# Attention scores of a pair of heads on the two row halves of TensorE, with q and k split once per pair

## The chip, the cores and the metric

The kernel runs on one core of one Trainium2 chip. The metric is the device time of one execution in microseconds (us); the time before is the median of three runs. TensorE (PE in the profile) multiplies, VectorE (DVE) and ScalarE (ACT) do elementwise work, and SyncE (SP) issues every transfer between HBM and the core.

## The reference, cut to what matters

```python
# batch 4, 8 heads, seq 768, head dim 64; sink 4, window 128
scores = scale * np.matmul(q, k.transpose(0, 1, 3, 2))
keep = is_sink | in_window                  # a band of 128 keys, and the first 4 keys
a = softmax(np.where(keep, scores, -1e9))
x = np.matmul(a, v)                         # (3072, 512) once the heads lie side by side
h = x @ w_in                                # 512 -> 2048
g = np.where(h >= 1, h, np.where(h <= -1, 0, (h + 1) ** 2 / 4))
x = g @ w_out                               # 2048 -> 512
logits = x @ phi                            # 32 slots; softmax over tokens, over slots
slots = softmax_over_tokens(logits).T @ x
out = softmax_over_slots(logits) @ experts(slots)     # 8 experts, w1 and w2
```

## The kernel before

**Attention** is cut into 96 steps m: 12 groups g of 256 query rows (3 to a batch), in each group 4 pairs of heads hp, in each pair 2 query tiles t of 128 rows. The pair number is k = 4g + hp = m // 2. A step makes a 128x272 score tile for each of its two heads a (16 sink keys and two blocks of 128 keys; 128x128 for the first tile of a batch): `st_s` on PE, `st_ttr` (mask and row minimum) on DVE, `st_exp` on ACT, a norm, transposes `st_pt`, and for each pair one `st_pv` that sums with V. In steps from FO on, `st_fold` adds one half of the band into the other, so that two transposes do instead of four and DVE, not ACT, copies them out.

**Scores.** q and k of a head come by one transfer into a `qkr` tile (64 rows of data; the array in HBM holds them twice, one copy under the other). For pairs with k < WH (9 before) a head's scores are one plain float32 matmul on the 64 rows, which the trace shows as two records (L490, "s<-qkr 64*128"). For the others the head is split: `qkh` holds the rounded high part of q and k on rows 0 to 63, and on rows 64 to 127 the low part of q beside the high part of k once more; `kl` holds the low part of k on all 128 rows. Then a head takes two single-pass matmuls over all 128 rows (L494 and L495). The split costs for each head a copy on ACT or DVE (`sp_hi`, L461 or L463) and two subtractions on DVE (`sp_ql` and `sp_kl`, both recorded at L292).

**MLP.** Unit n (96 of them) is one 128-row tile times one 512-wide block of w_in: `u_mm` (twelve 128x512 matmuls, L633), `u_r` on ACT, `u_a` and `u_g` on DVE, transposes `u_gt` (L659), and the logits `u_lg` (L678). w_in and w_out arrive as 64-bit words and are unpacked on ACT and DVE during the first 140 us. The experts follow as a tail of some 74 us.

**Order.** `Plan` simulates the engines with a planned cost for each step, and the order in which its steps start is the order of each engine's queue. `Plan.setup` charges PE a set-up of 0.15 or 0.2 when it goes from or to steps named in PARTS (those that use 32 or 64 columns of the array); steps s are not in PARTS. Where the plan sees PE without work before the first logits, or near the end, `filled` puts fill matmuls (L1380). A score tile takes one of two PSUM banks "S", given back by `st_exp`.

Of the kernel before, what the change touches and what calls it, by code (L numbers as in the profile page):

```python
# [172 lines left out]
def attn_moe_softmoe_kernel(ctx, tc, qk0, qk1, kt, qt, vt, vs, sizes,  # L173
# [117 lines left out]
    def minus(o, x, y):  # L291
        V.tensor_tensor(o, x, y, ALU.subtract)  # L292
# [117 lines left out]
    def at(shape, tag, bufs, dt=F32, nm=None):  # L410
        return att["pool"].tile(shape, dt, name=nm or tag, tag=tag, bufs=bufs)
# [5 lines left out]
    def load_qk(h):  # L417

        g, h8 = divmod(h, 8)
# [6 lines left out]
        qkr[8 * g + h8] = t  # L426
# [22 lines left out]
    def qk_tiles(hh):  # L449
        k, i = divmod(hh, 2)  # L450
        return qkh[k], kl[k], i, 528 if (k // 4) % GPB == 0 else 672

    def sp_hi(hh, e):

        k = hh // 2
        if hh % 2 == 0:
            qkh[k] = at([128, 2, 672], "qkh", 2, F32R, nm=f"qkh{k}")
            kl[k] = at([128, 2, 416], "kl", 2, F32R, nm=f"kl{k}")
        h, l, i, w = qk_tiles(hh)
        if e == "ACT":  # L460
            A.activation(h[:, i, 0:w], qkr[hh][:, 0:w], AF.Copy)  # L461
        else:
            V.tensor_copy(h[:, i, 0:w], qkr[hh][:, 0:w])  # L463

    def sp_ql(hh):
        h, l, i, w = qk_tiles(hh)
        minus(h[64:128, i, 0:256], qkr[hh][64:128, 0:256], h[64:128, i, 0:256].bitcast(F32))

    def sp_kl(hh):
        h, l, i, w = qk_tiles(hh)  # L470
        minus(l[:, i, 0:w - 256], qkr.pop(hh)[:, 256:w], h[:, i, 256:w].bitcast(F32))
# [12 lines left out]
    def st_s(m, a):  # L484
        g, hp, t, b, i, k0, n, nm = geom(m)
        k = 4 * g + hp
        s = pt([128, 512], "S", 2, nm=f"s{m}_{a}")
# [534 lines left out]
    NTW, XCAP, GCAP, RCAP, ARATE, WK0, WK1, OK0, OK1 = 7, 3, 6, 3, 0.947, -7.119, 1.613, 6.435, 1.902  # L1022
    PK0, AN0, AN1, GTO, LGO, RO, AO, PVO, PTO = 60.0, 1, 55, 2.818, 1.79, 0.87, 0.891, 1.256, 1.239
    CKO, SPO, BO, GR, LASTN, LGT, HC, SLACK, FM = 1.633, -0.108, -0.708, 14, 5, 1.124, 6, 0.044, 0.296
    CT0, CT1, QKR, WIK, HO, TWO, NPT, NEAR, WH = -1, 0.5, 3, -26, 0, 1, 3, 3, 9
    FO, PAIRED, LGD = 22, 1, 1.5
# [105 lines left out]
    def fast_path():  # L1132
# [27 lines left out]
        for k, (kind, j, c) in enumerate(pairs):  # L1160
            key = (WK0 + k * WK1) if kind == "w" else (OK0 + (k - n_w) * OK1)
            ld = op(f"ld_raw{k}", "DMA", 2.92, key - 4, cv_load, acq=["w8", "raw"])
            ab = op(f"abs{k}", "ACT", 1.06, key + BO, lambda k=k: cv_abs(k), [ld], acq=["cv"] if wide else [])
# [30 lines left out]
        lds, spl, vop, vsop = {}, {}, {}, {}  # L1194
# [12 lines left out]
        for m in range(NPAIR):  # L1207
            g, hp, t, b, i, k0, w, nm = geom(m)
            key = A_(m)
            wide_q = g % GPB != 0  # L1210
            if t == 0:
                sp = []
                for a in range(2):
                    hh = 8 * g + 2 * hp + a
                    l = op(f"ld_qk{hh}", "DMA", .66 if WHOLE(hh // 2) else .96 if wide_q else .73, key - 4, lambda hh=hh: load_qk(hh), acq=["qkr"])
                    if WHOLE(hh // 2):
                        sp.append([l])
                        continue
                    aq = ["qkh"] if a == 0 else []
                    spk = key + SPO  # L1220
                    h = op(f"qh{hh}", {"ACT": .64 if wide_q else .5, "DVE": .45 if wide_q else .37}, 0, spk,
                           lambda e, hh=hh: sp_hi(hh, e), [l], acq=aq, prior=[x[0] for x in sp])
                    q = op(f"ql{hh}", "DVE", .45, spk, lambda hh=hh: sp_ql(hh), [h])
                    kk = op(f"kl{hh}", "DVE", .6 if wide_q else .48, spk, lambda hh=hh: sp_kl(hh), [h])
                    op.free("qkr", [q, kk])
                    sp.append([h, q, kk])
                spl[g, hp] = sp
            ex, tt = [], []
            for a in range(2):
                whole = WHOLE(m // 2)  # L1230
# [3 lines left out]
                last_s = s  # L1234
# [233 lines left out]
```

## Time and profile before

| | before |
|---|---|
| median of three runs | 642.07 us (637.44 to 644.04) |
| profiled execution | 637.39 us |
| its span in the trace | 635.5 us (so 1.9 us lie around it) |
| PE busy | 616.9 us, 97% |
| DVE busy | 502.3 us, 79% |
| ACT busy | 412.3 us, 65% |

A busy PE in this profile is not a PE at its peak: a matmul's duration includes its way through the array, and matmuls overlap. What a matmul costs in a dense stream is the distance from its start to the start of the next one; that is what the rows further down are read for. PEld is PE's load of the stationary operand. In a name such as "128x512" the second number is the columns that stream; "64*128" is array rows times array columns in use.

### The profile page before, as it was taken

What the parts mean: (1) busy time and instruction counts of PE and PEld (TensorE: products, weight loads), DVE (VectorE), ACT (ScalarE), POOL (GpSimd) and SP (SyncE); (2) the same over time, 40 slices, a digit from 0 to 9 for tenths busy, and PEclk for the clock granted to TensorE, in tenths of its full rate; (3) what the DMA queues carried; (4) which work ended last, traced back from release to release, by engine and by line L of the source; (5) the groups of instructions that cost most, each with busy time, mean ns of one, the idle gap of its engine ahead of it and who ended that gap; (6) DMA issues with size and microseconds to landing.
All of it is one profiled execution on the core that took longest, in us unless ns stands there. A gap on an engine that the chain in (4) does not pass through costs nothing.

```text
span 635.5 us, 12324 instructions
## 1 busy us (share of the span) xinstructions
PE 616.9 (97%) x4420; PEld 453.3 (71%) x4420; DVE 502.3 (79%) x1561; ACT 412.3 (65%) x1175; POOL 3.3 (1%) x12
## 2 busy tenths in 40 slices
PE   8999999999999999999999999999999999999992
PEld 5667788777876778777877887886878867653452
DVE  6999999999989789878999998999998642455053
ACT  4998999888878667676776655676666433332143
POOL 0000000000000000000000000000000000010000
PEclk9999999999999999999999999999999999999997
DMA  8766384672611311421314123324230194879996
GB/s 274 231 194 218 124 281 145 219 262 99 210 47 48 112 36 36 136 65 47 104 44 122 52 64 94 88 83 132 60 109 27 36 426 154 312 300 342 418 382 221
DMA packets 34342, 100.92 MB, mean 159 GB/s; under 512 B 3808, under 2 KB 9952, under 8 KB 29664
## 3 DMA queue, kind: packets, MB, share of 16 engines
q1 hardware_dynamic: 34272, 100.04, 46.8%
q8 instruction: 37, 0.61, 0.4%
q14 instruction: 33, 0.27, 0.1%
HBM read 89.54 MB, written 10.49 MB: 157 GB/s over the span
## 4 chain that ended last, share of the span: by engine, by line


## 5 line engine op out<-in xcount | busy, mean ns | idle before, releaser
L633 PE MATMUL h<-winh,x 128*128 128x512 f32 x768 | 278.6, 407 | 0.0
L633 PEld LDWEIGHTS h<-winh,x 128*128 128x128 f32 x768 | 144.4, 188 | 34.6 <-issue 8.5
L633 PE MATMUL h<-winl,x 128*128 128x512 f32 x384 | 150.4, 392 | 0.0
L510 ACT ACTIVATE p<-s,st 128x272 f32<-128x272 f32 (+1 forms) x192 | 87.9, 463 | 24.2 <-DVE st L503 21.7
L638 ACT ACTIVATE r<-h 128x512 f32<-128x512 f32 x96 | 57.0, 595 | 48.2 <-PE h L633 27.9
L503 DVE CUSTOM_DVE_ANT_0 s<-s,nm 128x272 f32<-128x272 f32 (+1 forms) x192 | 77.6, 430 | 10.2 <-PE s L490 5.3
L633 PEld LDWEIGHTS h<-winl,x 128*128 128x128 f32 x384 | 72.6, 189 | 9.3
L666 ACT ACTIVATE gT<-gtp,one 128x512 f32<-128x512 f32 x96 | 65.7, 685 | 16.2 <-PE gtp L659 16.0
L653 DVE SCALAR_TENSOR_TENSOR gm<-r,gm 128x512 f32<-128x512 f32 x96 | 65.7, 687 | 1.1
L650 DVE TENSOR_SCALAR gm<-r 128x512 f32<-128x512 f32 x96 | 40.8, 427 | 25.0 <-ACT r L638 24.7
L659 PE MATMUL gtp<-ident_r,gm 128*128 128x128 f32 x384 | 58.7, 275 | 0.5 <-DVE gm L653 0.5
L461 ACT ACTIVATE qkh<-qkr 128x672 fp32r<-128x672 f32 (+1 forms) x61 | 44.0, 729 | 15.9 <-PE s L495 15.9
L659 PEld LDWEIGHTS gtp<-ident_r,gm 128*128 128x128 f32 x384 | 44.0, 141 | 12.3 <-issue 5.3
L598 PE MATMUL pv<-pT,v 128*64 128x128 f32 x704 | 49.0, 279 | 0.0
L494 PE MATMUL s<-qkh 128*128 128x272 f32 (+1 forms) x156 | 46.9, 318 | 0.2 <-ACT p L510 0.2
L292 DVE TENSOR_TENSOR kl<-qkr,qkh 128x416 fp32r<-128x416 f32 (+1 forms) x78 | 42.2, 541 | 0.6
L555 PE MATMUL pt<-ident_r,p 128*128 128x128 f32 x228 | 42.0, 279 | 0.2 <-ACT pT L568 0.2
L495 PE MATMUL s<-kl,qkh 128*128 128x272 f32 (+1 forms) x156 | 42.1, 287 | 0.0
L598 PEld LDWEIGHTS pv<-pT,v 128*64 128x64 f32 x704 | 37.5, 136 | 4.4 <-issue 1.6
L510 ACT ACTIVATION_READ_ACCUMULATOR p<-s,st 128x1 f32 x192 | 38.6, 201 | 0.0
L555 PEld LDWEIGHTS pt<-ident_r,p 128*128 128x128 f32 x228 | 28.4, 141 | 12.3 <-issue 3.7
L494 PEld LDWEIGHTS s<-qkh 128*128 128x128 f32 x156 | 29.4, 189 | 10.6 <-issue 8.4
(155 smaller groups left out, 933.9 us busy)
## 6 DMA issues: line engine op xcount, KB each, us to landing
w<-in_w SPq DMA_DIRECT2D x32, 1024.0 KB, 8.9
qkr<-in_qk SPq DMA_DIRECT2D x54, 336.0 KB, 3.0
raw<-in_w_in SPq DMA_DIRECT2D x8, 1024.0 KB, 6.3
raw<-in_w_out SPq DMA_DIRECT2D x8, 1024.0 KB, 6.0
qkr<-in_qk SPq DMA_DIRECT2D x24, 264.0 KB, 2.7
v<-in_vt SPq DMA_DIRECT2D x24, 256.0 KB, 3.2
out<-o SPq DMA_DIRECT2D x12, 512.0 KB, 7.0
wo<-cv SPq DMA_DIRECT2D x8, 512.0 KB, 3.4
```

Of the source, the lines that this page charges most:

```text
L292: V.tensor_tensor(o, x, y, ALU.subtract)
L461: A.activation(h[:, i, 0:w], qkr[hh][:, 0:w], AF.Copy)
L494: T.matmul(s[:, 0:n], q, qkh[k][:, a, 256 + k0:256 + k0 + n], start=True, stop=False)
L503: V.tensor_tensor_reduce(out=s, in0=s, in1=nm, op0=ALU.add, op1=ALU.min, scale=-0.125, scalar=3.0e38, accum_out=rs[m][:, a:a + 1])
L510: A.activation(p_sb[m][:, a, 0:n], s_ps.pop((m, a))[:, 0:n], AF.Exp, bias=rs[m][:, a:a + 1], scale=-1.0, accum_out=rs[m][:, 2 + a:3 + a])
L555: T.transpose(ps[:, nc_ * a + c, :], p[:, a, col:col + 128], ident)
L598: T.matmul(ps[64 * a:64 * a + 64, t, :], vch[b, ch][:, h * 64:h * 64 + 64], o[:, len(chunks) * a + c, :], start=False, stop=(c == len(chun ...
L633: T.matmul(hps[n], x[:, c, t, :], (win_h, win_l)[w][j][:, c, :], start=(k == 0), stop=(k == 11))
L638: A.activation(r, hps.pop(n), AF.Relu, bias=0.5, scale=0.5)
L653: V.scalar_tensor_tensor(gm[n], ru.pop(n), 1.0, gm[n], ALU.subtract, ALU.mult)
L659: T.transpose(ps[:, c, :], gm[n][:, c * 128:(c + 1) * 128], ident)
L666: A.activation(gT[n // 2][:, :, t * 128:t * 128 + 128], gtp.pop(n), AF.Identity, bias=one)
```

## The change

- A pair's two heads lie one under the other in HBM and in `qkr`: head 0 on rows 0 to 63, head 1 on rows 64 to 127. One transfer loads them, where there were two.
- The split is made once per pair on all 128 rows: one copy `sp_hi` into `qkh`, and one subtraction `sp_lo` of the whole width (672 or 528) into `kl`, which now holds the low parts of q and of k.
- `st_s` takes both heads in one step of PE, each on its half of the rows: high x high, high x low, low x high, for head 0 and head 1 in turn. That is six matmuls of 64 rows where there were four of 128. A step with k < WH takes one plain float32 matmul per head. The step takes both "S" banks at once.
- The plan costs a step .36 (split) or .47 (whole), where it had .251 or .46 for each head; set-up rules are as before.
- WH goes from 9 to 11, FO from 22 to 16, and the keys and limits of the plan get new values; from unit RAWN on, a place in the plan is ordered behind the last load of raw weights.

```diff
-        t = at([128, 672], "qkr", QKR, nm=f"qkr{h}")
-        w = 528 if gi == 0 else 672
-        src = qk0[b, h8 // 2, :, h8 % 2] if gi == 0 else qk1[b, gi - 1, h8 // 2, :, h8 % 2]
-        n = 64 if WHOLE(h // 2) else 128
-        SP.dma_start(t[0:n, 0:w], src[0:n])
+        t = qkr[k] = at([128, 672], "qkr", QKR, nm=f"qkr{k}")
+        SP.dma_start(t[:, 0:qk_width(k)], qk0[b, hp] if gi == 0 else qk1[b, gi - 1, hp])
...
-    def sp_ql(hh):
-        h, l, i, w = qk_tiles(hh)
-        minus(h[64:128, i, 0:256], qkr[hh][64:128, 0:256], h[64:128, i, 0:256].bitcast(F32))
-
-    def sp_kl(hh):
-        h, l, i, w = qk_tiles(hh)
-        minus(l[:, i, 0:w - 256], qkr.pop(hh)[:, 256:w], h[:, i, 256:w].bitcast(F32))
+    def sp_lo(k):
+        w = qk_width(k)
+        kl[k] = at([128, 672], "kl", 2, F32R, nm=f"kl{k}")
+        minus(kl[k][:, 0:w], qkr.pop(k)[:, 0:w], qkh[k][:, 0:w].bitcast(F32))
...
         if WHOLE(k):
-            r = qkr[2 * k + a][0:64]
-            T.matmul(s[:, 0:n], r[:, t * 128:t * 128 + 128], r[:, 256 + k0:256 + k0 + n], start=True, stop=True)
-            s_ps[m, a] = s
-            return
-        q = qkh[k][:, a, t * 128:t * 128 + 128]
-        T.matmul(s[:, 0:n], q, qkh[k][:, a, 256 + k0:256 + k0 + n], start=True, stop=False)
-        T.matmul(s[:, 0:n], q, kl[k][:, a, k0:k0 + n], start=False, stop=True)
-        s_ps[m, a] = s
+            terms = [(qkr[k], qkr[k])]
+        else:
+            terms = [(qkh[k], qkh[k]), (qkh[k], kl[k]), (kl[k], qkh[k])]
+        for x, (q, o) in enumerate(terms):
+            for a in range(2):
+                r = slice(64 * a, 64 * a + 64)
+                T.matmul(s_ps[m, a][:, 0:n], q[r, t * 128:t * 128 + 128], o[r, 256 + k0:256 + k0 + n],
+                         start=x == 0, stop=x == len(terms) - 1)
...
-                s = op(f"s{m}_{a}", "PE", (.46 if w > 128 else .22) if whole else .251, key, lambda m=m, a=a: st_s(m, a),
-                       spl[g, hp][a] + ([last_s] if last_s else []),
-                       acq=["S"], rel=["qkr"] if whole and t else ["qkh"] if t and a else [])
+            c = (.47 if whole else .36) * (1 if w > 128 else .5)
+            s = last_s = op(f"s{m}", "PE", c, key, lambda m=m: st_s(m), sp + ([last_s] if last_s else []),
+                            acq=["S", "S"], rel=["qkr" if whole else "qkh"] if t else [])
```

**Where the order moves.** First PE, in unit n = 41 (tile h_3776 before, h_3705 in the change), where a step with split heads stands between the two halves of the unit's twelve h matmuls; s_0 and s_1 are the score tiles of the two heads. Before:

```order
L633 MATMUL h_3776<-winh_264,x_3048 128x512
L494 MATMUL s_0_3793<-qkh_3633 128x128
L495 MATMUL s_0_3793<-kl_3634,qkh_3633 128x128
L494 MATMUL s_1_3798<-qkh_3633 128x128
L495 MATMUL s_1_3798<-kl_3634,qkh_3633 128x128
L633 MATMUL h_3776<-winh_264,x_3048 128x512
```

In the change, at the same place:

```order
L624 MATMUL h_3705<-winh_264,x_3018 128x512
L486 MATMUL s_0_3726<-qkh_3565 128x128
L486 MATMUL s_1_3727<-qkh_3565 128x128
L486 MATMUL s_0_3726<-kl_3570,qkh_3565 128x128
L486 MATMUL s_1_3727<-kl_3570,qkh_3565 128x128
L486 MATMUL s_0_3726<-qkh_3565,kl_3570 128x128
L486 MATMUL s_1_3727<-qkh_3565,kl_3570 128x128
L624 MATMUL h_3705<-winh_264,x_3018 128x512
```

The neighbours stay what they were; four matmuls of 128 rows have become six of 64 rows, which go to head 0 and head 1 in turn.

Second PE, in unit n = 4 (h_793 and h_796), where a step with whole heads stands between the halves. Before:

```order
L633 MATMUL h_793<-winh_607,x_305 128x512
L490 MATMUL s_0_807<-qkr_684 128x272
L490 MATMUL s_1_813<-qkr_776 128x272
L633 MATMUL h_793<-winh_607,x_305 128x512
L633 MATMUL h_793<-winl_608,x_305 128x512
```

In the change:

```order
L624 MATMUL h_796<-winh_585,x_291 128x512
L486 MATMUL s_0_811<-qkr_567 128x272
L486 MATMUL s_1_812<-qkr_567 128x272
L624 MATMUL h_796<-winh_585,x_291 128x512
L624 MATMUL h_796<-winl_586,x_291 128x512
```

The rows read alike; the two matmuls now read the upper and the lower half of one tile qkr_567, where they read the upper halves of two tiles.

Third DVE, near unit n = 40, where one pair is split (qkh_3499, kl_3500 and two qkr tiles before; qkh_3411, kl_3429 and one qkr tile in the change). Before, with other work between the rows left out:

```order
L463 CAST qkh_3499<-qkr_3412 128x528
L292 TENSOR_TENSOR qkh_3499<-qkr_3310,qkh_3499 64x256
L292 TENSOR_TENSOR kl_3500<-qkr_3310,qkh_3499 128x272
...
L292 TENSOR_TENSOR qkh_3499<-qkr_3412,qkh_3499 64x256
...
L292 TENSOR_TENSOR kl_3500<-qkr_3412,qkh_3499 128x272
```

In the change:

```order
L494 ISA s_0_3392,st_3413<-s_0_3392,nm_162 128x272
L494 ISA st_3413 128x1
L494 ISA s_1_3393,st_3413<-s_1_3393,nm_162 128x272
L494 ISA st_3413 128x1
L292 TENSOR_TENSOR kl_3429<-qkr_3040,qkh_3411 128x528
L515 TENSOR_TENSOR p_3427<-p_3427 128x2x128
```

Five instructions of DVE for the pair have become one, and the pair's one high copy stands on ACT.

## Rows read from the trace of the kernel before

**Rows 1.** Page, part 1: busy us, share of the span, instructions.

```profile
PE 616.9 (97%) x4420; PEld 453.3 (71%) x4420; DVE 502.3 (79%) x1561; ACT 412.3 (65%) x1175; POOL 3.3 (1%) x12
```

**Rows 2.** Stretches: length, busy us and instructions by engine, clock, DMA share, GB/s.

```profile
31.80:47.70 15.90, 15.90 (x88) 10.89 (x88) 15.84 (x43) 15.90 (x44) 0.00 (x0) 1.00 0.60 194
...
95.00:127.00 32.00, 32.00 (x242) 26.12 (x242) 30.27 (x85) 29.96 (x84) 0.00 (x0) 1.00 0.55 184
...
254.00:286.00 32.00, 32.00 (x226) 24.43 (x225) 25.32 (x85) 22.50 (x73) 0.00 (x0) 1.00 0.34 100
```

**Rows 3.** Waits of PE: who waited for whom, us in total, times, longest.

```profile
PE fill_lg L1380 <- DVE ident_r L230: 1.6, 1, 1.6
...
PE s L494 <- ACT p L510: 0.2, 1, 0.2
```

**Rows 4.** Timeline of PE (start us, us, what): last h of first and last unit.

```profile
44.52 0.40 PE L633 MATMUL h<-winh,x 128*128 128x512 f32 x1
...
561.16 0.40 PE L633 MATMUL h<-winh,x 128*128 128x512 f32 x1
```

**Rows 5.** Timeline of PE: a split step between gtp transposes and h.

```profile
304.44 0.60 PE L659 MATMUL gtp<-ident_r,gm 128*128 128x128 f32 x4
304.80 0.37 PE L494 MATMUL s<-qkh 128*128 128x272 f32 x1
305.01 0.29 PE L495 MATMUL s<-kl,qkh 128*128 128x272 f32 x1
305.13 0.28 PE L494 MATMUL s<-qkh 128*128 128x272 f32 x1
...
305.38 0.39 PE L633 MATMUL h<-winh,x 128*128 128x512 f32 x1
305.61 0.39 PE L633 MATMUL h<-winl,x 128*128 128x512 f32 x1
```

**Rows 6.** Timeline of PE: one whole head, then a whole step between two h.

```profile
48.94 0.72 PE L490 MATMUL s<-qkr 64*128 64x272 f32 x2
49.59 0.44 PE L589 MATMUL pv<-sTt,vs 96*128 96x128 f32 x2
...
63.62 0.40 PE L633 MATMUL h<-winh,x 128*128 128x512 f32 x1
63.95 1.18 PE L490 MATMUL s<-qkr 64*128 64x272 f32 x4
65.06 0.50 PE L633 MATMUL h<-winh,x 128*128 128x512 f32 x1
65.40 0.40 PE L633 MATMUL h<-winl,x 128*128 128x512 f32 x1
```

**Rows 7.** Timeline of PE: pv, logits, then a split step.

```profile
260.14 1.09 PE L598 MATMUL pv<-pT,v 128*64 128x128 f32 x16
261.16 0.64 PE L678 MATMUL lg<-gT,wphi 128*32 128x256 f32 x8
261.73 0.39 PE L494 MATMUL s<-qkh 128*128 128x272 f32 x1
261.96 0.29 PE L495 MATMUL s<-kl,qkh 128*128 128x272 f32 x1
```

**Rows 8.** Groups by line and shape: busy us, mean ns, idle before: the splits.

```profile
L292 DVE TENSOR_TENSOR qkh<-qkr,qkh 64x256 fp32r<-64x256 f32 x78 | 33.0, 423 | 2.4
L461 ACT ACTIVATE qkh<-qkr 128x672 fp32r<-128x672 f32 x43 | 32.3, 764 | 9.9 <-PE s L495 9.9
L292 DVE TENSOR_TENSOR kl<-qkr,qkh 128x416 fp32r<-128x416 f32 x54 | 31.7, 586 | 0.3
...
L292 DVE TENSOR_TENSOR kl<-qkr,qkh 128x272 fp32r<-128x272 f32 x24 | 10.5, 439 | 0.3
```

**Rows 9.** Timeline of DVE: the fourth x, and the first kl.

```profile
42.86 0.42 DVE L610 TENSOR_TENSOR x<-pv,x 128x256 fp32r<-128x256 f32 x1
...
82.41 0.58 DVE L292 TENSOR_TENSOR kl<-qkr,qkh 128x416 fp32r<-128x416 f32 x1
```

More of the change, by code (lines that the diff above doesn't have):

```diff
@@ L447, in cv_vsl, with qk_width, sp_hi @@
         vsb[b] = o
[L449 to L458, printed above, removed]
[L459 removed]
+    def qk_width(k):
+        return 528 if (k // 4) % GPB == 0 else 672
+    def sp_hi(k, e):
+        w = qk_width(k)
+        qkh[k] = at([128, 672], "qkh", 2, F32R, nm=f"qkh{k}")
         if e == "ACT":
[L461 removed]
+            A.activation(qkh[k][:, 0:w], qkr[k][:, 0:w], AF.Copy)
         else:
[L463 to L471 removed]
+            V.tensor_copy(qkh[k][:, 0:w], qkr[k][:, 0:w])
+    def sp_lo(k):
+        w = qk_width(k)
+        kl[k] = at([128, 672], "kl", 2, F32R, nm=f"kl{k}")
+        minus(kl[k][:, 0:w], qkr.pop(k)[:, 0:w], qkh[k][:, 0:w].bitcast(F32))
     def geom(m):
@@ L482, in geom, with st_s @@
         return g, hp, t, b, i, 144 * t, 272, mk.get("nm2")
-    def st_s(m, a):
+    def st_s(m):
         g, hp, t, b, i, k0, n, nm = geom(m)
         k = 4 * g + hp
-        s = pt([128, 512], "S", 2, nm=f"s{m}_{a}")
+        for a in range(2):
+            s_ps[m, a] = pt([128, 512], "S", 2, nm=f"s{m}_{a}")
         if WHOLE(k):
-            r = qkr[2 * k + a][0:64]
-            T.matmul(s[:, 0:n], r[:, t * 128:t * 128 + 128], r[:, 256 + k0:256 + k0 + n], start=True, stop=True)
-            s_ps[m, a] = s
-            return
-        q = qkh[k][:, a, t * 128:t * 128 + 128]
-        T.matmul(s[:, 0:n], q, qkh[k][:, a, 256 + k0:256 + k0 + n], start=True, stop=False)
-        T.matmul(s[:, 0:n], q, kl[k][:, a, k0:k0 + n], start=False, stop=True)
-        s_ps[m, a] = s
+            terms = [(qkr[k], qkr[k])]
+        else:
+            terms = [(qkh[k], qkh[k]), (qkh[k], kl[k]), (kl[k], qkh[k])]
+        for x, (q, o) in enumerate(terms):
+            for a in range(2):
+                r = slice(64 * a, 64 * a + 64)
+                T.matmul(s_ps[m, a][:, 0:n], q[r, t * 128:t * 128 + 128], o[r, 256 + k0:256 + k0 + n],
+                         start=x == 0, stop=x == len(terms) - 1)
     def st_ttr(m, a):
@@ L1020, in attn_moe_softmoe_kernel @@
     tw = {}
[L1022 to L1026, printed above, removed]
+    NTW, XCAP, GCAP, RCAP, ARATE, WK0, WK1, OK0, OK1 = 7, 3, 6, 3, 0.947, -6.74, 1.613, 8.405, 1.186
+    PK0, AN0, AN1, GTO, LGO, RO, AO, PVO, PTO = 60.0, 5, 53, 2.818, 1.79, 0.724, 0.872, 1.256, 1.239
+    CKO, SPO, BO, GR, LASTN, LGT, HC, SLACK, FM = 1.898, -0.224, -0.708, 14, 5, 1.042, 6, 0.044, 0.352
+    CT0, CT1, QKR, WIK, HO, TWO, NPT, NEAR, WH = -1, 0.5, 3, -25, 0, 5, 3, 2, 11
+    FO, PAIRED, LGD, RAWN = 16, -7, 1.5, 15
     WHOLE = lambda k: k < WH
@@ L1191, in fast_path @@
                 odone[j] = prev_o
-        lds, spl, vop, vsop = {}, {}, {}, {}
+        vop, vsop = {}, {}
         pvs, xop = {}, {}
@@ L1209, in fast_path @@
             key = A_(m)
-            wide_q = g % GPB != 0
+            wide_q, k, whole = g % GPB != 0, 4 * g + hp, WHOLE(4 * g + hp)
             if t == 0:
[L1212 to L1219, printed above, removed]
-                    spk = key + SPO
[L1221 to L1227, printed above, removed]
+                l = op(f"ld_qk{k}", "DMA", .96 if wide_q else .73, key - 4, lambda k=k: load_qk(k), acq=["qkr"])
+                sp = [l]
+                if not whole:
+                    spk = key + SPO
+                    h = op(f"qh{k}", {"ACT": .64 if wide_q else .5, "DVE": .45 if wide_q else .37}, 0, spk,
+                           lambda e, k=k: sp_hi(k, e), [l], acq=["qkh"])
+                    sp = [h, op(f"ql{k}", "DVE", .85 if wide_q else .7, spk, lambda k=k: sp_lo(k), [h], rel=["qkr"])]
@@ L1313, in fast_path @@
             a = op(f"a{n}", "DVE", .34, n + AO, lambda n=n: u_a(n), [r],
-                   acq=["w8", "gm"] if gm_tile(n)[1] == 0 else [], prior=[aop[x] for x in aop if gm_tile(x)[0] == gm_tile(n)[0]][:1])
+                   acq=["w8", "gm"] if gm_tile(n)[1] == 0 else [], prior=[aop[x] for x in aop if gm_tile(x)[0] == gm_tile(n)[0]][:1]
+                   + ([raw_op[len(pairs) - 1]] if n >= RAWN else []))
             aop[n] = a
@@ L1429, in pack @@
         a = np.concatenate(parts, axis=-1)
-        a = np.concatenate([a, a], axis=2)
-        return a.reshape(B, H // 2, 2, 2 * D, -1).transpose(0, 1, 3, 2, 4)
+        return a.reshape(B, H // 2, 2 * D, -1)
     qk0 = np.ascontiguousarray(pack(0))
```

8 lines of the change are left out of this document (3 added, 5 removed).

## The prediction, made before the changed kernel ran

> **What bounds the kernel now.** I read the page first, then the stretches, the waits of PE, and last the timeline of PE step by step. The page has PE at 97% of the span, DVE at 79% and ACT at 65% [rows 1]. The stretches divide the run: from 31.8 to 47.7 us DVE is busy 15.84 of 15.90 us and ACT all of it, unpacking w_in and doing the first softmaxes; later DVE and ACT have air (25.32 and 22.50 of 32 us), while PE shows 32.00 of 32.00 throughout, at a granted clock of 1.00, the 2.4 GHz level [rows 2]. So the start is bound by DVE and ACT, and all between the end of the first unit (44.5 us) and of the last (561.2 us) [rows 4] by PE. The waits agree: PE's longest wait is 1.6 us, once, and for a score bank it waits 0.2 us, once [rows 3].
>
> A busy PE says nothing of how densely it is fed, so I price by distances between starts. A matmul of h follows the one before after 0.23 us [rows 5]. A single-pass score matmul of 272 columns takes 0.37 / 3 = 0.125 us (305.01 to 305.38), and a transpose (0.94 - 4 x 0.125) / 4 = 0.11 us (304.44 to 305.38, four transposes and four score matmuls) [rows 5]. I wrote out PE's order of before and priced each entry so, with the price of switches below: from the end of the first unit to the end of the last it comes to 512 of the 516.7 us that the trace has [rows 4]. PE's own stream is the time, and real waits are at most 4.7 us. So I price the order of the change in the same way.
>
> **What a step on 64 rows costs beside its streaming.** The kernel before has such steps already: the whole heads. Two of their records cost 0.65 us from start to next start (48.94 to 49.59) and four cost 1.11 us (63.95 to 65.06), so a record streams (1.11 - 0.65) / 2 = 0.23 us [rows 6]. The rest is not streaming. The step starts 0.33 us after the last h instead of 0.23 (63.62 to 63.95): 0.10 us. Of its 1.11 us 4 x 0.23 = 0.92 is streaming, 0.19 is not: about 0.10 before the second record, as its operand's load lies bare, and 0.09 on leaving. The next h follows its first after 0.34 instead of 0.23 (65.06 to 65.40): 0.11 us, again a bare load [rows 6]. A step on 64 rows between two h so costs 0.40 us more than it streams. A step on all 128 rows costs nothing of the kind: gtp, four score matmuls and h follow one another without a gap [rows 5]. After logits, which use 32 columns of the array, the same price is paid by a full-width step: the second score matmul starts 0.23 us after the first instead of 0.125 [rows 7]. It is a price for changing the form of the array, in either direction.
>
> The Trainium skill says the same on its page "TensorEngine Tiling (Array Packing)", section Key Properties: changing the tiling mode, not just the tile, drains TensorE. The rows agree, with 0.10 us of drain and, of which the page doesn't speak, 0.10 of bare load; by the drain alone the sum would be that of rival 3, and by the page's table of theoretical speedups alone (2x for a contraction of 64 or less) that of rival 2.
>
> **The change part by part, after the first unit.**
>
> *Split steps.* Before, 78 steps of four matmuls, 312 x 0.125 = 39.0 us. In the change 74 steps (two pairs more are whole), six matmuls each, in three rounds of two. No row shows two row halves at work at once. Side by side, a round is 0.125 and a step 0.375; one after another, 0.75. The nearest rows are those of pv, on two column halves: 16 records of 128 columns in 1.02 us (260.14 to 261.16), 0.064 each, where a transpose of 128 columns on the full array takes 0.11 [rows 5, 7]. These run in twos. I take side by side: 74 x 0.375 = 27.8 us, -11.2.
>
> The Trainium skill, "TensorE: Matmul & The Clock Gate", section "Part 3: Packing small matmuls", has matmuls on distinct row groups run concurrently, starts some 4 ns apart. No run here shows it for rows; for column halves the rows above do.
>
> *Whole steps.* Before, 7 steps of four records, 28 x 0.23 = 6.44 us; now 11 steps of two rounds, 22 x 0.23 = 5.06 us: -1.4. The others lie before the first unit's end.
>
> *Switches.* Counted over PE's order after the first unit, changes of form go from 262 to 389. A score step now begins with one 85 times (9 before) and ends with one 85 times (9 before). 24 of these entries follow logits, pv or a 32-row transpose, where a full-width step had to switch as well, and cost nothing new [rows 7]. What is new is 52 entries from the full array at 0.10 + 0.10 = 0.20 us, 10.4 us, and 75 exits to it. An exit to h costs 0.09 + 0.11 = 0.20 [rows 6]; 46 of the 84 to the full array are such. The others go mostly to transposes, for whose load no row stands here; between 0 and 0.11 I take half: 75 x 0.175 = 13.1 us. Together +23.5.
>
> *Transposes and fills.* FO = 16 folds six steps more: 12 transposes less, 12 x 0.11 = -1.3. Two fills near the end fewer: -0.4.
>
> Sum: -11.2 - 1.4 + 23.5 - 1.3 - 0.4 = **+9.2 us**.
>
> *DVE and ACT.* The two subtractions per head, 33.0 + 31.7 + 10.5 = 75.2 us of DVE [rows 8], become 37 of 672 or 528 columns. From 272 to 416 columns the row rises 0.439 to 0.586 us, 1.02 ns a column, so 25 x 0.85 + 12 x 0.70 = 29.6 us: 45 us of DVE less, and 26 copies of ACT at up to 0.764 us [rows 8]. I cost this at nothing. The first kl stands at 82.41 us [rows 9]; the start, where DVE is the bound, has whole heads alone and gets none of it. Later PE's stream covers it. At most the 4.7 us of waits could go.
>
> *Loads.* Half the transfers for q and k, and for split pairs half the bytes; in the start, where heads are whole, the bytes stay. SP issues fewer, nothing waits for it: zero.
>
> *The two banks.* A score step now needs both "S" banks, so it waits for the second head's exp, with all of h and pv queued behind it on PE. Before, that wait was 0.2 us in the run [rows 3] and the plan counts both banks; zero, with up to 3 us as a bound.
>
> *The start.* PE's own work before the end of the first unit falls by 4.8 us, and fills rise from 51 to 71; neither counts, as PE waits there for the fourth x on DVE (42.86 us [rows 9]). Priced by rows, the work ahead of that x on DVE's order is 1.0 us more. I take zero, with -2 and +1 as bounds. Between 45 and 130 us PE's order is up to 4 us shorter in the change, which DVE (30.27 of 32 us busy [rows 2]) may not let through: up to +4.
>
> The plan knows nothing of the switches: its set-up leaves s out, so it placed score steps where h, not logits, stand beside them.
>
> Against the profiled execution's own 637.39 us that is 646.6. That execution is at the low end of the runs; on their median, 642.07, it is 651.3, **651 us**. A difference under 1% (642 +/- 6.4) can hardly be told from none here.
>
> **The rivals.**
>
> 1. *The halves don't run side by side.* If the matmuls go one after another, split steps cost 74 x 0.375 = 27.8 us more and whole steps 11 x 2 x 0.23 = 5.1: 684 us. If only the loads of the operands do (0.11 us for 128 columns, as transposes are spaced [rows 5]), a round is 0.22: 74 x 3 x 0.095 = 21 us more, 672 us. For it: no row shows row halves. Against: the column halves [rows 7]. Chance 0.10 together.
>
> 2. *The switch isn't charged*, the other side. The saved streaming is 14.3 us, so the change gains as soon as one of the 127 extra switches costs under 14.3 / 127 = 0.113 us. With none charged it is 642 - 14 = 628 us; this would need the charge to hang on one idle half, not on the 64 rows. Against: the logits keep all four of their 32-column groups at work, and the step behind them is charged all the same [rows 7]. Chance 0.08. The table of speedups in the Trainium skill, named above, would give about this.
>
> 3. *Half charged.* The drain stays, but the second half's load covers the bare one: 127 x 0.095 = 12.1 us, 642 - 2 = 640 us. Against: both halves' loads come at once, after the drain. Chance 0.07.
>
> **How the numbers follow.** My forecast has 0.75; its own range is 645 (waits and start give 6 back) to 659 (DVE holds the early gain, banks wait). 648.5 is 1% over: of the 0.75 I put 0.54 above and 0.21 below. Slower by over 1%: 0.54 + 0.10 = 0.64. Within 1%: 0.21 + 0.07 = 0.28. Faster: 0.08. The range 638 to 664 holds my forecast and rival 3 and leaves out rivals 1 and 2 (0.18).
>
> **What would show it.** In the profile after: six score matmuls in pairs a few ns apart, rounds 0.125 us apart (0.25: rival 1); the score step 0.33 us after an h, its second round some 0.23 us after the first, the h behind it 0.34 before the next (0.23 there: rival 2; 0.33 but no late second round: rival 3). DVE's busy time falls by about 40 us and the span doesn't. The first unit ends between 42.5 and 45.5 us; if much earlier, the start was misread, and if PE waits by more than some us between 45 and 560 us, so was the bound.

## The result and the profile after

| | before | after |
|---|---|---|
| median of 20 runs each | 641.49 us (637.44 to 645.79) | 644.87 us (644.06 to 646.25) |
| profiled execution | 637.39 us | 644.81 us |
| first unit's last h, last unit's last h | 44.52, 561.16 us | 44.16, 568.31 us |

The change is slower: ratio 1.0059, 95% interval 1.0040 to 1.0078, some 3.4 us. The forecast had the right sign, but +9.2 us. Two things catch the eye: the profiled executions lie 7.4 us apart, the medians only 3.4; and the runs of before spread over 8 us, those of the change over 2.

The page of the change, part 1 (against [rows 1]): DVE has 35 us less, ACT 16, PE 6.5 more.

```profile
PE 623.4 (97%) x4574; PEld 440.6 (69%) x4574; DVE 466.9 (73%) x1451; ACT 396.6 (62%) x1137; POOL 3.3 (1%) x12
```

Its stretches, in the columns of [rows 2]. In the first ACT is as full as before, DVE and PE stand still for some 0.4 and 0.3 us; later DVE has more air than before, and PE has none, as before.

```profile
31.80:47.70 15.90, 15.58 (x90) 10.78 (x91) 15.46 (x40) 15.90 (x43) 0.00 (x0) 1.00 0.55 193
95.00:127.00 32.00, 32.00 (x247) 24.89 (x244) 29.22 (x74) 25.97 (x72) 0.00 (x0) 1.00 0.61 193
254.00:286.00 32.00, 32.00 (x234) 23.05 (x233) 21.55 (x71) 22.67 (x73) 0.00 (x0) 1.00 0.21 66
```

Its timeline of PE (start us, us, what), against [rows 4]: the last h of the first and of the last unit.

```profile
44.16 0.39 PE L624 MATMUL h<-winh,x 128*128 128x512 f32 x1
...
568.31 0.40 PE L624 MATMUL h<-winh,x 128*128 128x512 f32 x1
```

From the one to the other are 524.15 us, where before has 516.64: +7.5. The start is 0.4 us shorter, the tail 0.3 longer. So between the two profiles the whole difference lies where the prediction put it.

The same view, a split step between transposes and h, against [rows 5]:

```profile
306.63 0.60 PE L650 MATMUL gtp<-ident_r,gm 128*128 128x128 f32 x4
307.16 0.39 PE L486 MATMUL s<-qkh 64*128 64x272 f32 x2
307.39 0.29 PE L486 MATMUL s<-kl,qkh 64*128 64x272 f32 x2
307.52 0.28 PE L486 MATMUL s<-qkh,kl 64*128 64x272 f32 x2
307.73 0.50 PE L624 MATMUL h<-winh,x 128*128 128x512 f32 x1
308.07 0.39 PE L624 MATMUL h<-winl,x 128*128 128x512 f32 x1
```

Each row is a round of two matmuls, one for each head (x2); in the records they start 3 ns apart here, and at most 12 ns apart in all 74 split steps. The second round comes 0.23 us after the first, the third 0.13 after that, h 0.21 after it, and the next h after 0.34. A whole step between two h, against [rows 6]:

```profile
61.04 0.40 PE L624 MATMUL h<-winh,x 128*128 128x512 f32 x1
61.37 0.73 PE L486 MATMUL s<-qkr 64*128 64x272 f32 x4
62.03 0.50 PE L624 MATMUL h<-winh,x 128*128 128x512 f32 x1
62.36 0.39 PE L624 MATMUL h<-winl,x 128*128 128x512 f32 x1
```

It starts 0.33 us after the h and lasts 0.66, where it lasted 1.11: two rounds of 0.23 and 0.20 of switching.

### The profile page after: what moved, and what is told of

It reads as the page before. It is cut to its first block, busy times and chain, and to the rows that moved or that the text cites. A ratio compares the mean times of both kernels' runs of the same rounds, so it can differ in the third digit from the quotient of the medians.

```text
span 642.9 us, 12374 instructions
## 1 busy us (share of the span) xinstructions
PE 623.4 (97%) x4574; PEld 440.6 (69%) x4574; DVE 466.9 (73%) x1451; ACT 396.6 (62%) x1137; POOL 3.3 (1%) x12
## 4 chain that ended last, share of the span: by engine, by line
PE 87%; ACT 4%; DVE 4%; DMA 2%; issue 0%; SPq 0%; ACTq 0%
PE h L624 43%; PE s L486 8%; PE gtp L650 7%; PE pv L589 6%; PE lg L669 4%; PE pt L546 4%; PE eg L735 3%; PE w2p L944 2%; PE w1p L906 2%; DMA raw<-in_w_out 1%; PE pv L580 1%; DMA raw<-in_w_in 1%; PE wotp L377 1%; ACT raw L332 1%; PE lt L681 1%; ACT p L501 1%
## 5 line engine op out<-in xcount | busy, mean ns | idle before, releaser
L624 PE MATMUL h<-winh,x 128*128 128x512 f32 x768 | 283.0, 414 | 0.2 <-ACT r L629 0.2
L555 DVE TENSOR_TENSOR pT<-pt,tri 128x256 f32<-128x256 f32 x68 | 28.6, 421 | 25.1 <-PE pt L565 14.6
L546 PEld LDWEIGHTS pt<-ident_r,p 128*128 128x128 f32 x216 | 26.3, 141 | 15.8 <-issue 3.9
L453 ACT ACTIVATE qkh<-qkr 128x672 fp32r<-128x672 f32 (+1 forms) x35 | 25.4, 725 | 18.9 <-PE s L486 18.6
L525 DVE TENSOR_SCALAR p<-p,st 128x144 f32<-128x144 f32 (+2 forms) x142 | 36.1, 296 | 1.2
L570 ACT ACTIVATE sTt<-pt 96x128 fp32r<-96x128 f32 x68 | 18.5, 272 | 28.9 <-PE pt L565 12.8
L515 DVE TENSOR_TENSOR p<-p 128x256 f32<-128x256 f32 x68 | 28.2, 414 | 5.9 <-ACT p L501 5.5
```

Source lines behind the costliest of these rows:

```text
L525: V.tensor_scalar(p[:, a, 0:n], p[:, a, 0:n], st[:, 4 + a:5 + a], None, ALU.mult)
L546: T.transpose(ps[:, nc_ * a + c, :], p[:, a, col:col + 128], ident)
L624: T.matmul(hps[n], x[:, c, t, :], (win_h, win_l)[w][j][:, c, :], start=(k == 0), stop=(k == 11))
```

## The experiments

Times are medians; the ratio is to the kernel before, run in turn on the same chip. "Start" is the time of the first unit's last h in the profiled execution, "body" the time from there to the last unit's last h. The change was not run again beside e2, e3, e7, e8 and e10. Their distance from it is taken between samples in which the median of before itself moved from 640.07 to 641.49, so some 1.5 us of it may be the sample; their start and body come from the profiles.

| | median us (range), runs | ratio [95%] | start, body us |
|---|---|---|---|
| e1 before, subtractions 32 wide | 638.38 (634.77 to 644.12), 12 | 0.9973 [0.9948, 0.9999] | 47.03, 515.15 |
| e2 change, subtraction twice | 647.42 (646.57 to 649.35), 6 | 1.0106 [1.0082, 1.0130] | 44.52, 525.74 |
| e3 change, plan knows the switches | 642.65 (640.72 to 646.15), 12 | 1.0035 [1.0011, 1.0059] | 44.90, 520.18 |
| e4 before once more | 641.02 (638.12 to 647.68), 12 | 1.0008 [0.9980, 1.0036] | 50.19, 517.00 |
| e5 before, pair in one tile | 635.74 (633.37 to 639.03), 12 | 0.9937 [0.9914, 0.9960] | 42.19, 516.88 |
| e6 before, ring of four tiles | 638.31 (637.20 to 639.88), 12 | 0.9975 [0.9955, 0.9994] | 45.77, 516.42 |
| e7 change, transfers cut in two | 649.72 (646.37 to 652.24), 6 | 1.0151 [1.0112, 1.0189] | 48.48, 523.73 |
| e8 change, 41 fills | 644.93 (644.21 to 646.53), 6 | 1.0084 [1.0051, 1.0117] | 44.33, 523.68 |
| e9 before, split scores on 64 rows | 663.37 (662.45 to 668.22), 6 | 1.0383 [1.0339, 1.0427] | 45.78, 540.99 |
| e10 change, head after head | 645.65 (645.12 to 646.88), 7 | 1.0094 [1.0062, 1.0127] | 44.65, 524.25 |
| e11 e5 and one transfer for a pair | 633.38 (632.87 to 635.34), 6 | 0.9895 [0.9860, 0.9929] | 41.98, 515.45 |

### Where does before lose what its profile doesn't show? (e4)

> The kernel before once more, word for word, for a second profile and for how far two samples of the same program lie apart. The ratio is 1.000 by both theories, with an interval that shows what a measurement of this kernel can tell. If its profiled execution lies near 641 us, not at 637.4, then its longer stretches against the first profile show where the usual run of before loses its 4 us: theory A has them between units 8 and 95, in waits of PE ended by DVE or ACT instructions; theory B has them in the start or in the tail, or spread evenly over PE's stream.

This profiled execution took 644.99 us. Its body is 517.00 us, 0.4 from the first profile's; its start is 5.7 us longer. Its timeline of PE, first unit's last h:

```profile
50.19 0.39 PE L633 MATMUL h<-winh,x 128*128 128x512 f32 x1
```

Its transfers (engine, count, KB each, median us from issue to landing): the first raw weights, issued between 2 and 5.5 us, then q and k issued between 8 and 13 us.

```profile
raw<-in_w_in SPq DMA_DIRECT2D x2, 1024.0 KB, 9.3
...
qkr<-in_qk SPq DMA_DIRECT2D x2, 132.0 KB, 8.0
```

The same two rows in the first profile of before:

```profile
raw<-in_w_in SPq DMA_DIRECT2D x2, 1024.0 KB, 6.6
...
qkr<-in_qk SPq DMA_DIRECT2D x2, 132.0 KB, 4.1
```

The waits of PE and ACT in the first 52 us of e4 (who for whom: us in total, times, longest):

```profile
PE s L490 <- DMA qkr<-in_qk: 3.2, 3, 1.4
...
ACT cv L328 <- DMA raw<-in_w_in: 4.5, 2, 3.2
```

In the first profile these are 0.5 and 1.5 us. And the stretches of e4, columns as in [rows 2]:

```profile
30.00:32.00 2.00, 0.67 (x3) 0.50 (x2) 1.88 (x7) 1.57 (x4) 0.00 (x0) 0.73 1.03 265
32.00:34.00 2.00, 2.00 (x6) 1.56 (x6) 1.83 (x5) 2.00 (x8) 0.00 (x0) 0.50 0.62 215
34.00:36.00 2.00, 2.00 (x6) 1.48 (x5) 0.41 (x2) 0.21 (x2) 0.00 (x0) 0.50 0.06 23
36.00:38.00 2.00, 2.00 (x8) 1.44 (x7) 0.00 (x0) 0.84 (x2) 0.00 (x0) 0.56 0.00 0
```

Read downwards: PE stands still for q and k, its granted clock falls to the 1.2 GHz level (0.50), it works through its h and transposes at half speed, and DVE and ACT, the bound of the start, stand still behind it. So the 5.7 us begin with late loads. It is no single case: e1's profile, whose start ends at 47.03 us, has such a stretch as well (30 to 32 us: clock 0.51, after a wait of PE of 1.2 us for q and k). Of 76 runs of before in these experiments, the 17 above 642 us all have a mean clock of 0.983 to 0.991, and of the 17 below 639 us 15 have 0.993 or 0.994; the change's 20 runs all have 0.993 or 0.994. Theory B's place, the start, is right for this execution, and theory A's is wrong. That the 4 us by which before's median exceeds its profile lie there in the other runs too is what their clocks suggest; no trace of them shows it.

### Is DVE's load worth anything? (e1, e2)

e1, before without most of the subtractions:

```diff
-        minus(h[64:128, i, 0:256], qkr[hh][64:128, 0:256], h[64:128, i, 0:256].bitcast(F32))
+        minus(h[64:128, i, 0:32], qkr[hh][64:128, 0:32], h[64:128, i, 0:32].bitcast(F32))
-        minus(l[:, i, 0:w - 256], qkr.pop(hh)[:, 256:w], h[:, i, 256:w].bitcast(F32))
+        minus(h[:, i, 256:288], qkr.pop(hh)[:, 256:288], h[:, i, 256:288].bitcast(F32))
...
-        T.matmul(s[:, 0:n], q, kl[k][:, a, k0:k0 + n], start=False, stop=True)
+        T.matmul(s[:, 0:n], q, qkh[k][:, a, 256 + k0:256 + k0 + n], start=False, stop=True)
```

> The kernel before with DVE relieved and PE left alone: both subtractions of a split head are made over 32 columns only (the one for k in place, in the high tile), so the low parts are missing from the scores and the second score matmul reads the high part again. PE's, ACT's and SP's instructions and their order stay those of before. By the rows of before (0.423, 0.586 and 0.439 us for 256, 416 and 272 columns, 1.02 ns a column) 156 subtractions save about 78 x 0.23 + 54 x 0.39 + 24 x 0.24 = 45 us of DVE, what the change saved. Theory A: what the sum left out is this relief; PE waits for DVE in most executions of before (its profiled one, 637.4 us, was one of the fastest, its median is 641.5), and the change took those waits away. Then this kernel is 3 to 5 us faster than before on the median (ratio 0.992 to 0.995) and its runs lie closer together than before's 637 to 646. Theory B: the spread of before's runs has nothing to do with DVE's load, and PE's stream is the time in all of them: ratio 0.998 to 1.002, the spread as before.

DVE fell by 38.0 us, the median by 1.9, the body by 1.5; the runs spread as far as before's. A small gain, and no steadiness. The 1.5 us alone would not show that DVE is its cause: e11's body is as short (515.45 us) with DVE's load as it was. e2, the change with DVE loaded again:

```diff
-        minus(kl[k][:, 0:w], qkr.pop(k)[:, 0:w], qkh[k][:, 0:w].bitcast(F32))
+        x = qkr.pop(k)
+        for _ in range(2):
+            minus(kl[k][:, 0:w], x[:, 0:w], qkh[k][:, 0:w].bitcast(F32))
```

> The change with the load given back to DVE: each subtraction of a split pair is made twice, 37 instructions more on DVE at 0.70 to 0.85 us (estimated from the rows of before), some 29 us of its 45 us relief. PE's order stays that of the change. Theory A (the relief is worth some 2 us in the profiles and some 4 on the median): 2 to 4 us slower than the change (ratio to before 1.009 to 1.012), with PE's longest waits on DVE instructions. Theory B (PE's stream is the time, DVE is hidden): no more than 1 us from the change's 1.005 to 1.006.

DVE rose by 24.8 us, the median by 2.5, the body by 1.6. The waits of PE in its body:

```profile
PE h L626 <- ACT r L631: 1.1, 1, 1.1
PE eg L737 <- DVE ek L728: 0.4, 1, 0.4
```

The change itself has one such wait, of 0.2 us. So loading DVE again costs the change some 1.5 us of its body, and these waits show where; that relieving it gave before as much fits e1, but isn't shown by it. Theory A is right in kind, and far too small for the median.

### What is it that makes the change's start steady? (e5 to e8, e11)

The change does one thing that the prediction passed over: a qkr tile holds a pair, and the ring still has three tiles. Before, three heads could be in flight or in use; now six. e5 does this on the kernel before:

```diff
-        t = at([128, 672], "qkr", QKR, nm=f"qkr{h}")
...
-        n = 64 if WHOLE(h // 2) else 128
-        SP.dma_start(t[0:n, 0:w], src[0:n])
+        if WHOLE(h // 2):
+            t = qkr[h - 1] if h % 2 else at([128, 672], "qkr", QKR, nm=f"qkr{h}")
+            r = slice(64 * (h % 2), 64 * (h % 2) + 64)
...
-            r = qkr[2 * k + a][0:64]
+            r = qkr[2 * k + a][64 * a:64 * a + 64]
```

> The kernel before with one edit: for whole pairs the two heads lie in one qkr tile, head 0 on rows 0 to 63 and head 1 on rows 64 to 127, so that the three tiles of the ring hold six heads where they held three. Bytes, transfers and the order on every engine stay those of before; only the transfers of the start may be issued earlier. What e4 showed: before's slow executions lose all their time ahead of the end of the first unit (50.2 us against 44.5 in the first profile, and 517.0 against 516.7 us from there to the end of the last), after q and k came late (issued between 9 and 12 us, landed after 8.0 us instead of 4.1) and PE stood still and its granted clock fell to 0.50 between 32 and 36 us. Theory 'lead': the change made the start robust by its deeper ring. Then this kernel's first unit ends at 42 to 45 us in nearly every execution, its median is 637 to 639 us, its runs lie within some 3 us of one another at a clock of 0.993 to 0.994 (ratio to before 0.993 to 0.997). Rival 'fills or order': the start of the change is robust by its other order and its 71 instead of 51 fill matmuls, and the ring is nothing: ratio 0.998 to 1.002, the runs spread over 637 to 646 with clocks down to 0.986.

Median 4.3 us below before; the start ends at 42.19 us. But e5 does more than its text says. Head 1 is now multiplied on the upper half of the rows, so the two heads run side by side, as in the change, in most of the whole steps that take both at once. Its timeline of PE, against [rows 6]:

```profile
60.84 0.40 PE L637 MATMUL h<-winh,x 128*128 128x512 f32 x1
61.16 0.73 PE L494 MATMUL s<-qkr 64*128 64x272 f32 x4
61.82 0.50 PE L637 MATMUL h<-winh,x 128*128 128x512 f32 x1
```

Such a step lasts 0.66 us instead of 1.11. All whole steps together take 2.9 us less of PE ahead of the first unit's end and 1.9 us less behind it; in the body of this profile a wait of 1.5 us for a score bank, which before doesn't have, hides that. So the 4.3 us are not the ring's alone. Transfers that waited for a tile now go out earlier: the fourth raw block is issued at 13.77 us, where before has 19.79. The runs are closer together, but one of twelve still took 639.03 at a clock of 0.985. e6 leaves the heads on one half and gives the ring one tile more:

```diff
-        t = at([128, 672], "qkr", QKR, nm=f"qkr{h}")
+        t = at([128, 672], "qkr", 4, nm=f"qkr{h}")
```

> The kernel before with four qkr tiles instead of three, nothing else: one head more can be loaded ahead. Theory 'lead': a smaller part of what e5 brings, ratio 0.995 to 0.999, fewer runs at a clock below 0.992. Rival 'fills or order': as before, 0.998 to 1.002, with the same spread.

It is 0.25% below before, with an interval that ends under 1, and has runs within 2.7 us of one another. So the ring counts, by some 1.6 us for one tile more. e7 leaves the change its ring and cuts the transfers:

```diff
-        SP.dma_start(t[:, 0:qk_width(k)], qk0[b, hp] if gi == 0 else qk1[b, gi - 1, hp])
+        src = qk0[b, hp] if gi == 0 else qk1[b, gi - 1, hp]
+        for r in ([slice(0, 64), slice(64, 128)] if WHOLE(k) else [slice(0, 128)]):
+            SP.dma_start(t[r, 0:qk_width(k)], src[r])
```

> The change with the one transfer of a whole pair cut in two, rows 0 to 63 and rows 64 to 127, as many and as large as before's; ring, order and fills stay those of the change. Rival 'transfers' (fewer and larger transfers are what makes the change's start robust): the runs spread as before's do, clocks down to 0.988, median 2 to 4 us above the change's (ratio to before 1.009 to 1.012). Theory 'lead' and the other rival: no more than 1 us from the change (1.004 to 1.007), the runs within 3 us of one another.

4.8 us slower than the change, more than the rival expected and against theory 'lead', 4.3 us of it in the start (48.48 against 44.16 us). Its wait of ACT for the first raw weights:

```profile
ACT cv L328 <- DMA raw<-in_w_in: 5.2, 1, 5.2
```

In the change that wait is 2.1 us. SP needs 0.47 to 0.60 us to issue a transfer of 64 rows and 0.33 to 0.47 for one of 128; the first raw block goes out at 4.82 us instead of 3.08 and the second at 6.46 instead of 4.07. e8 asks whether it is the fills instead:

```diff
             n = int((o.start - t - FM) / cost) if a else 0
+            n = n * 5 // 7 if o.start < first else n
```

> The change with 41 instead of 71 fill matmuls ahead of the first logits, each group of fills cut to five sevenths; all else stays. Rival 'fills' (the change's start is robust because 20 more fills keep PE's granted clock at 1.00): with fewer than before's 51 the runs spread over some 8 us, with clocks down to 0.985, median 2 to 5 us above the change's (1.009 to 1.014). Theory 'lead': PE waits no longer for q and k, its gaps stay short, and the time stays within 1 us of the change's (1.004 to 1.007).

644.93 us, and a start of 44.33 us against the change's 44.16. The ratio, 1.0084, lies above what theory 'lead' expected (1.007) and below the rival's 1.009, as before ran 1.4 us faster in this sample; its interval and the change's overlap, so no effect of the fills can be told. The runs lie within 2.3 us of one another: the steady start doesn't need the 30 fills. e11 takes both to the kernel before, ring and transfer; as in e5, whole heads run side by side, and the split scores stay as they are (against e5):

```diff
         if WHOLE(h // 2):
-            t = qkr[h - 1] if h % 2 else at([128, 672], "qkr", QKR, nm=f"qkr{h}")
-            r = slice(64 * (h % 2), 64 * (h % 2) + 64)
+            if h % 2:
+                t = qkr[h - 1]
+            else:
+                t = at([128, 672], "qkr", QKR, nm=f"qkr{h}")
+                SP.dma_start(t[:, 0:w], qp0[b, h8 // 2] if gi == 0 else qp1[b, gi - 1, h8 // 2])
```

> e5 (before with the two heads of a whole pair in one tile) and one thing more: a whole pair comes in one transfer of 128 rows, from an array that holds its heads one under the other, as in the change. The order of all other instructions is before's, split heads are loaded as before. Theory 'transfers' (e7: cutting these transfers in two cost the change 4.8 us, as the first raw weights land later): the start gains once more, the first unit ends some 2 us ahead of e5's 42.2, though DVE may not let all of it through behind it; median 633 to 635 us, ratio to before 0.987 to 0.993. Rival 'ring alone': what e7 lost hangs on the change's order, and this kernel is as e5, 0.992 to 0.996.

633.38 us, its runs within 2.5 us of one another: 1.0% below before, and the fastest kernel here. The start's end is only 0.2 us ahead of e5's profile, so "the start gains once more" was wrong there. The body is 1.4 us shorter than e5's, whose wait of 1.5 us it doesn't have. (The profiled execution is the slowest of the six, at 635.34.) How much of the change's own steadiness belongs to ring, to transfer and to the whole heads side by side is not settled: e7 shows that without the transfer the other two aren't enough in the change's order, e6 that a longer ring helps without either. No run here has the heads side by side with the ring and the transfers of before.

### The price of a switch, and the two row halves (e9, e3, e10)

e9 changes nothing but the form of before's split steps:

```diff
-        q = qkh[k][:, a, t * 128:t * 128 + 128]
-        T.matmul(s[:, 0:n], q, qkh[k][:, a, 256 + k0:256 + k0 + n], start=True, stop=False)
-        T.matmul(s[:, 0:n], q, kl[k][:, a, k0:k0 + n], start=False, stop=True)
+        q = qkh[k][0:64, a, t * 128:t * 128 + 128]
+        T.matmul(s[:, 0:n], q, qkh[k][0:64, a, 256 + k0:256 + k0 + n], start=True, stop=False)
+        T.matmul(s[:, 0:n], q, kl[k][0:64, a, k0:k0 + n], start=False, stop=True)
```

> The kernel before with its split score matmuls cut to rows 0 to 63 of their operands: as many matmuls, of the same columns, in the same order, one after another on the same half of the array; the product of the low part of q with the high part of k, which lies on the other rows, is left out. All that changes on PE is the form of 78 steps. Theory 'switch': PE's order then has 146 changes of form more between the ends of the first and the last unit, at 0.09 + 0.10 us each 27.8 us, so that stretch goes from 516.7 to 544 us, and the ratio to before is 1.039 to 1.046; the first of the matmuls starts 0.33 us after an h, the second 0.23 us after it. Rival 'not charged': the time stays within 0.3% of before's.

Ratio 1.0383, just under the range expected, the body 24.3 us longer for 146 switches. Interval by interval, all of it lies in the score steps and the first interval behind each. Its timeline of PE shows a step between two h:

```profile
309.24 0.40 PE L633 MATMUL h<-winh,x 128*128 128x512 f32 x1
309.57 0.39 PE L494 MATMUL s<-qkh 64*128 64x272 f32 x1
309.80 0.28 PE L495 MATMUL s<-kl,qkh 64*128 64x272 f32 x1
309.92 0.28 PE L494 MATMUL s<-qkh 64*128 64x272 f32 x1
310.04 0.28 PE L495 MATMUL s<-kl,qkh 64*128 64x272 f32 x1
310.25 0.50 PE L633 MATMUL h<-winh,x 128*128 128x512 f32 x1
310.59 0.39 PE L633 MATMUL h<-winl,x 128*128 128x512 f32 x1
```

0.33, 0.23, 0.12, 0.12, 0.21, 0.34: the streaming of a full-width step, and 0.10 + 0.11 + 0.09 + 0.11 us for the form alone. On one half of the rows, matmuls follow one another at 0.12; in the change two go in that time. Of the missing 3.5 us (27.8 expected) some 1.4 are a price set too high: 27 of the steps are followed by transposes, whose first two starts then lie 0.165 us apart instead of 0.11, so that the load costs 0.05 there and not 0.10. Most of the rest are waits of before that the longer step swallows: four steps grow by less than 0.15 us, or shrink, where their like grow by 0.3 to 0.4.

e3 lets the plan know the price (an excerpt; the plan's keys change with it, and WH falls from 11 to 10, so two steps more are split):

```diff
+        if self.score(o):
+            return 0.2
+        if self.score(p):
+            return 0.0 if o.name.startswith(self.PARTS) and o.name[:2] != "pv" else 0.15 if o.name[0] != "h" else 0.2
         if not p.name.startswith(self.PARTS):
             return 0.0
```

> The change with a plan that knows of the switches: a score step is charged 0.2 us where it begins and 0.15 or 0.2 where it ends, as pv and logits are, steps s behind logits and pv are put ahead, and the plan's keys and limits have new values; what is computed is the same. In PE's order the changes of form fall from 419 to 378; 54 score steps instead of 24 now stand behind steps of 32 or 64 columns. Theory 'switch': 41 switches at 0.09 + 0.1 us each are 7.9 us less of PE's stream, all of it between the ends of the first and the last unit: some 637 us where the change has 645, ratio to before 0.990 to 0.996. Rival 'not the switch': if the switch is no price of its own but PE was waiting for something else in the change, or if the steps now placed behind logits come too late for what needs them, the time stays within 2 us of the change's (1.002 to 1.009).

The body fell by 4.0 us, the median by 2.2. Between the last h of unit 28 and that of unit 80 the order has 28 switches less and some 2.5 us less of streaming, 7.8 us by price; the trace has 285.3 us there where the change has 292.5, 7.2 less. The rest is lost elsewhere in the body, most of it in one new wait of PE:

```profile
PE wpp L404 <- ACT wot L397: 2.2, 1, 2.2
```

So the price holds in this stretch. By it 41 switches less are 8 us of PE's stream; half of that is lost again, and e3 stays behind before.

e10 sets the six matmuls in another order:

```diff
-        for x, (q, o) in enumerate(terms):
-            for a in range(2):
+        for a in range(2):
+            for x, (q, o) in enumerate(terms):
```

> The change with the six matmuls of a split step in another order: the three terms of head 0, then the three of head 1. Steps with whole heads are as they were. Theory 'side by side, in order': matmuls go to the array in order, so the three of head 0 follow one another at 0.125 us on rows 0 to 63, and only the first of head 1 shares the array with the last of head 0: five rounds where there were three, 74 x 2 x 0.125 = 18.5 us, some 663 us, ratio to before 1.033 to 1.040. Rival 'never side by side, or nothing gained': if pairs of row halves brought nothing, the time stays at the change's 645 (1.005 to 1.008); if the halves never share the array in this order, 74 x 3 x 0.125 = 27.8 us, 673 us (1.05).

The theory misses: the body is 524.25 us, as the change's. The rival's 645 us came out to within 1 us, but not for its reason, that row halves bring nothing. Its timeline of PE:

```profile
303.20 0.40 PE L486 MATMUL s<-qkh 64*128 64x272 f32 x2
303.43 0.29 PE L486 MATMUL s<-kl,qkh 64*128 64x272 f32 x2
303.55 0.30 PE L486 MATMUL s<-qkh,kl 64*128 64x272 f32 x2
```

The instructions stand as qkh, kl, qkh-kl for head 0 and then the same for head 1, and yet the first terms start as a pair (8 to 10 ns apart in the records of this step, at most 17 in all), then the second ones, then the third. The rows name the tile but not the head; that the two of a pair belong to the two heads follows from the kernel, which has each term once for a head. So each half of the rows takes its own matmuls in order, and one half doesn't wait for the other's. The Trainium skill says otherwise on its page "TensorE: Matmul & The Clock Gate", section "Step-by-step: what each phase is for": only weight loads are pulled ahead, matmuls stay in program order. Here the first matmul of head 1, fourth in the program, starts 0.22 us ahead of the second of head 0; the run decides.

## Why the prediction was off

**What held.** PE's stream is the time of the body, and a step on 64 rows pays for changing the array's form on entering and leaving. The rows of after and e9 have every distance that the prediction named: 0.33 us after h, 0.23 to the second round, about 0.125 to the third, 0.34 behind the next h. For leaving to transposes no row stood there, and I took half of 0.11; the records of after have 0.165 instead of 0.11, so the half was right by luck. Row halves run side by side, so rival 1 is out; the switches are charged (e9: 24.3 us, where half the price would have given 14), so rivals 2 and 3 are out. The Trainium skill's rule from "TensorEngine Tiling (Array Packing)", section Key Properties, that a change of mode drains the engine, is borne out by e9's 24.3 us; the drain it names is half of what a switch costs. The first unit ended inside the stated 42.5 to 45.5 us. DVE fell by 35 us; the prediction names 45 in one place and about 40 in another. The subtractions went as its sum has them, from 75.2 to 29.7 us, and all rows of DVE together add up to 44 us less. But neighbouring rows of DVE overlap, on average by some 0.06 us, so the busy time, in which overlaps count once, falls by less (as in e1 and e2).

**The step "I cost this at nothing", on DVE and ACT.** Mis-sized by somewhat over 1 us. The body grew by 7.5 us where the sum has 9.2. (Profiles of the same two orders have 516.4 to 517.0 us, in before, e4 and e6, and 523.7 to 524.2, in the change, e7 and e8.) Some 0.5 us of that belong to another term, the split steps: 12 of them, before and after, have 128 columns, and such a step is 0.09 us shorter than I priced it in the change, 0.05 in before. The rest are waits that went. The relief of DVE is one cause (e2 gives back 1.6 us, with its waits in view; e1 takes 1.5 off before); the longer stream is another, since e9 loses waits with DVE's load as it was. How the rest divides between the two is not shown: the list of PE's waits between 50 and 565 us, which has long ones only, falls from 0.9 to 0.2 us. The text had the bound, "At most the 4.7 us of waits could go", and chose its lower end.

**The step "on their median, 642.07, it is 651.3", with zero for the loads and zero for the start behind it.** This is the larger failure. I added the 4.7 us between before's profile and its median to the change as well, as if they were a property of the chip. They are before's own: late q, k and raw weights in its start (seen in e4, and by their clocks likely in the other slow runs). The change's median lies 0.06 us above its profile, so 4.6 of the miss of 6.4 us (651.3 against 644.87) come from there, and the other 1.8 from the body, the start and the tail. What I had written on loads, "nothing waits for it", was wrong: in before's first profile PE already waits 0.5 us for q and k, and ACT 1.5 us for raw weights; in e4 it is 3.2 and 4.5. That "in the start, where heads are whole, the bytes stay" was true and beside the point: the bytes stayed, but the change makes one transfer of two and has twice the heads in the same ring, and a start that hangs on when loads land answers to both (e6 for the ring, e7 for the transfers; e5 and e11 have the whole heads side by side as well). The start also frees tiles sooner when whole steps are shorter, since SP's loads of q and k wait for PE's scores (29.3 us in the first 60 of before); of PE's shorter work there the text said that it doesn't count, and no run tests that alone. The warning was in the views that I had: before's three runs spread over 6.6 us, and its profile was the lowest of them. A profile at the low end says that something in the kernel varies; the question was what, and whether the change touches it.

**Left open.** Why the first raw weights and the q and k behind them land later in some executions (9.3 against 6.6 us, 8.0 against 4.1), with the same instructions; and, as said, how ring, transfer and the shorter whole steps share the change's steady start.

## What to carry to other kernels

Before adding a forecast difference to a median, ask why the median isn't the profile: profile several executions, find the stretch in which they differ, and see whether the change touches it. Count what a change of layout does to buffers and transfers, not to bytes alone; here side effects, twice the heads in the ring and half the transfers, were worth 7 us on the kernel before, together with whole heads side by side (e11): about as much as the change lost in its body. And a matmul form that uses part of the array is priced by its neighbours: here 0.2 us for entering, 0.2 for leaving to h, 0.15 to a transpose, unless the step beside it has to switch as well.

## What the runs showed of the hardware

- Two 64-row matmuls on the two row halves start at most 12 ns apart in the change, 17 in e10, and each half keeps its own order: written head after head, six matmuls take the same three rounds (e10).
- Changing between full-width and 64-row matmuls costs some 0.09 to 0.10 us before the first matmul and 0.10 before the second, in both directions; 0.05 before the second where it is a transpose of 128 columns (e9: 24.3 us for 146 switches, 0.17 each with the waits that went).
- While PE waited 1.33 us for q and k, its granted clock fell from 1.00 to 0.50, and it was 0.50 from 32 to 36 us with PE busy throughout; h matmuls started 0.43 us apart there instead of 0.23 (e4).
- A transfer of 64 rows holds SP's queue as long as or longer than one of 128 rows (0.47 to 0.60 against 0.33 to 0.47 us; e7 and the change, first 50 us).
